# Attention and MLP on one core: a third span's loads into an unused tile, elementwise work moved off GpSimd, a new opening order

## The chip, the core and the metric

The kernel runs on one core of a Trainium2 chip. A core has a matrix engine (TensorE, "PE" in the profile; its weight loads are "PEld"), three engines for elementwise work (VectorE "DVE", ScalarE "ACT", GpSimd "POOL") and SyncE ("SP"), which here only issues DMA transfers. Each engine works through its own queue of instructions in order. The metric is the device time of one execution in microseconds. The median of three runs is 311.8 us (311.51 to 313.07).

## What is computed

Sliding-window attention with a linear bias by distance, then a layer norm and a two-layer MLP with a residual. Batch 8, 8 heads, 576 positions, head size 64, so that a token has 512 features and the MLP 2048 hidden ones.

```
scores = scale * q @ k.T                    # per batch and head, 576 x 576
mask   = (rel >= 0) & (rel < 128)           # rel = query position - key position
attn   = softmax(where(mask, scores - slope[h] * |rel|, -1e9))
x      = heads side by side of (attn @ v)   # 8 x 576 x 512
xn     = (x - mean) / sqrt(var + 1e-6) * g_ln
out    = x + relu(xn @ w_ch1) @ w_ch2
```

## The kernel before, in words

The 4608 tokens are 36 blocks of 128. For a block the kernel turns q and k so that the head size lies on the partitions, makes the scores of the block with itself and with the block before it (line 771), takes the exponential on ScalarE (L819), masks by a product on VectorE (L826) or, for the first five blocks, adds a bias by a matmul beforehand (L787), multiplies with v (L847) and normalizes (L864, L868). The result is layer-normed, turned (L945 on TensorE for the first blocks, DMA transposes later) and enters the MLP as columns of a chunk. Chunks have 3, 3, 2 and then seven times 4 blocks. A chunk's first layer multiplies with w1 (L1244), a relu brings it into `ht` (L1257 on VectorE, L1259 on ScalarE), and the second layer multiplies with w2 (L1278 in the first three chunks). From the fourth chunk on the second layer is made by a seven-product scheme on halves (`seven`: products L1031, sums and differences of h and of the weights L1021 and L991), and in the last two chunks the first layer too (`fours`: products L1160, differences of x L1136, copies of partial results L1171 and L1173, joining additions L1183, a relu in place L1190, a relu from the accumulator L1218). Their sums of weights (L1117) are made late in the run.

`ht` is a ring of two tiles: chunk 0 uses the first, chunk 1 the second, and so on.

**The opening.** q and k of the first six blocks come in three "spans" of two blocks each, as 32-bit values over SyncE's DMA queue (L519): spans 0 and 1 in halves of four heads (256 KB a piece), span 2 as whole pieces (512 KB). They land in `qs` and `ks`, rings of two tiles, so span 2 takes the tiles of span 0 and its load waits until their casts are done. A cast (L666 on ScalarE, L668 on VectorE or GpSimd) makes them 16-bit pairs, TensorE turns them (L686), and VectorE or ScalarE evicts the turned tiles (L695, L697). v (L535) and the weights (L590, L592) come over GpSimd's DMA queue, which casts on the way; each issue is an instruction in GpSimd's own queue, behind its casts. While TensorE has nothing to do in the first 24 us, the program gives it small matmuls on a constant (L1328).

**What sets the order.** The program first lists all work as tasks: the engines that may do a task, a cost for each, dependences, a value `v` that says when it is due. A planner (`Plan.run`) then goes through time, gives every free engine the available task with the lowest value, takes the engine that would end it first where a task may go to several, and emits the instructions in the order found. Tables adjust this by hand: PRI adds to a task's value, HOLD keeps it back until a time, PICK says which engines may take it, QUEUE gives the order of the GpSimd DMA queue and of what is tied to it, and SHARES says how the planner splits the DMA between the two queues. So a change of a table or of one task's engines moves the order on all engines.

The value of a landing tile is a `Ring`: entry k takes tile k modulo the ring's size, its writers wait for the readers of the entry that had the tile before, and an entry can be pinned to a tile of its own:

```
def link(self):
    n = len(self.tiles)
    at = {self.turn(k): k for k in self.first if k not in self.pins}
    for k, tasks in self.first.items():
        if k in self.pins:
            continue
        for t in tasks:
            t.deps += self.readers.get(at.get(self.turn(k) - n), [])
```

Of the kernel before, what the change touches and what calls it, by code (L numbers as in the profile page):

```python
# [10 lines left out]
FP16 = mybir.dt.float16  # L11
FP32 = mybir.dt.float32
AF = mybir.ActivationFunctionType
ALU = mybir.AluOpType
# [41 lines left out]
class Plan:  # L56
# [10 lines left out]
        (True, 512): (0.83, 0.28), (True, 256): (0.75, 0.2), (True, 2048): (0.7, 0.4),  # L67
# [187 lines left out]
def kernel(  # L255
# [86 lines left out]
    mmix = sb("mmix", [P, 4, 2, 2 * P], FP16)  # L342
    mnew = sb("mnew", [P, 4, 2, 2 * P], FP16)
    w1sb = [sb(f"w1sb{m}", [P, NKB, CH], FP16) for m in range(CB)]
    w2sb = [sb(f"w2sb{m}", [P, CB, d_model], FP16) for m in range(CB)]

    single = any(i not in SPANS and i - 1 not in SPANS for i in range(LOAD_CAST))
    q32 = ring("q32", 2, [P, H, D if single else 1], FP32)
    k32 = ring("k32", 2, [P, H, D if single else 1], FP32)
    v32 = ring("v32", min(4, V_CAST), [P, H, D], FP32)  # L350
    qk16 = ring("qk16", 5, [P, 2, d_model], FP16)
    vx = ring("vx", 7 if V_CAST > 4 else 9, [P, H, VD], FP16, FAR)
    qkt = ring("qkt", 6, [P, 2, HP, P], FP16, FAR)
    qs = ring("qs", 2, [P, H, 2 * D], FP32)
    ks = ring("ks", 2, [P, H, 2 * D], FP32)
    qs16 = ring("qs16", 2, [P, H, D, 2], FP16)
    ks16 = ring("ks16", 2, [P, H, D, 2], FP16)
    probs = ring("probs", 3, [P, 4, 2, 2 * P], FP16)
    xb = ring("xb", 4, [P, CB, d_model], FP16)
    xs = ring("xs", 3, [P, d_model], FP16)  # L360
    xt = ring("xt", 3, [P, NKB, CH], FP16)
    ht = ring("ht", 2, [P, NFB, CH], FP16)
    ot = ring("ot", 3, [P, 2, d_model], FP32)
    gcol = sb("gcol", [P, NKB], FP32)
    st = ring("st", 4, [P, nc.vector.BN_STATS_DIM], FP32)
    mv = ring("mv", 4, [P, CB, nc.vector.BN_AGGR_DIM], FP32)
# [148 lines left out]
    def load_span(name, src, r, n, i, v, h0=0, h1=H):  # L515
        (_, _, b, s0), = where(i)

        def emit(e, bank):
            nc.sync.dma_start(  # L519
                out=r[n][:, h0:h1, :],  # L520
                in_=src[b, h0:h1, s0 : s0 + 2 * P, :].rearrange("h (p t) d -> p h (t d)", t=2),
            )
        share = (h1 - h0) / H
        t, d = plan.transfer(f"{name}{i}", "SP", 0.6, 0.05 + 1.7 * share + (0.25 if name in ("qs", "qs0") and i == 0 else 0.0), share, emit, (), v)
        if i < 4:
            d.lat = 1.05 if i else 0.6 if h0 == 0 else 0.9
        r.writes(n, t)
        return d
# [71 lines left out]
    def attention(i):  # L600
# [54 lines left out]
        if i in span_of:  # L655
            n = span_of[i]
            if SPANS[n] == i:
                evs, casts = [[], []], {}
                for (a, x), (landed, h0, h1) in span_load[n].items():
                    r_, w_ = ((qs, qs16), (ks, ks16))[a]  # L660

                    def e_c(e, b, r_=r_, w_=w_, n=n, h0=h0, h1=h1):
                        dst = w_[n][:, h0:h1, :, :].rearrange("p h d t -> p t h d")
                        src = r_[n][:, h0:h1, :].rearrange("p h (t d) -> p t h d", t=2)
                        if e == "ACT":
                            nc.scalar.activation(out=dst, in_=src, func=AF.Copy)  # L666
                        else:
                            (nc.vector if e == "DVE" else nc.gpsimd).tensor_copy(out=dst, in_=src)  # L668
                    f = (h1 - h0) / H
                    cs = add(  # L670
                        f"cT{i}.{a}{x}", pick(f"cs{a}{x}", "POOL", POOL=0.12 + 1.26 * f, ACT=0.22 + 1.18 * f, DVE=0.1 + 0.7 * f),
                        e_c, [landed], av(i, 0.1 * a + 0.2 * x),
                    )
                    r_.reads(n, cs); w_.writes(n, cs)
                    for y in range(2) if f == 1 else (x,):
                        casts[a, y] = cs
# [333 lines left out]
    def seven(c, relu, v0):  # L1010
# [8 lines left out]
        def sums(name, h, out, in0, in1, op, deps, v):  # L1019
            def emit(e, b):  # L1020
                (nc.vector if e == "DVE" else nc.gpsimd).tensor_tensor(out=out, in0=in0, in1=in1, op=op)  # L1021
            return add(f"{name}{c}.{h}", pick1(name, 2 * c + h, "DVE", DVE=0.69, POOL=1.45), emit, deps, v)
# [83 lines left out]
    def first_sums():  # L1106
# [3 lines left out]
        for m in range(2):  # L1110
# [4 lines left out]
            for n, (dst, x, y, op) in enumerate(((s1, a21, a22, ALU.add), (s2, s1, a11, ALU.subtract), (a21, a11, a21, ALU.subtract), (s4, a12, s2, ALU.subtract))):  # L1115
                def emit(e, b, dst=dst, x=x, y=y, op=op):
                    (nc.vector if e == "DVE" else nc.gpsimd).tensor_tensor(out=dst, in0=x, in1=y, op=op)  # L1117
                need = prev[-1:] + scaled[m :: 2] + free
                if n == 2:
                    need = need + plain_all[m + 2]  # L1120
                prev.append(add(f"sumW{m}.{n}", pick1("sumW", 2 * n + m, "POOL DVE", DVE=0.75, POOL=1.45), emit, need, FIRST[BOTH] / CB * SPAN - BEFORE - 12.0 + n))
# [247 lines left out]
```

## Time and profile before

| what | before |
|---|---|
| median of three runs | 311.8 us (311.51 to 313.07) |
| the profiled execution's own time | 312.74 us |
| its span, first to last instruction | 311.0 us |
| mean granted TensorE clock | 0.992 |
| first w1 matmul (L1244) starts | 26.65 us |
| busy in 235 to 291 us: PE, DVE, ACT, POOL | 53.40, 44.15, 22.62, 20.62 of 56 us |
| relus in place (L1190): GpSimd, VectorE | 10 of 1562 ns, 14 of 342 ns |
| differences of x (L1136): GpSimd, VectorE | 6 of 1272 and 1378 ns, 2 of 400 ns |
| loads of q and k spans, 256 KB, issue to landing | 4.9 and 4.6 us |
| load of the third span's k, 512 KB | 10.4 us |

The page cuts the span into 40 slices of 7.8 us and gives for each engine the busy share in tenths (9 is 90% or more); PEclk is the clock that TensorE was granted, in tenths of full speed. A row of a timeline has the start, the duration, the engine, the line, the operation, its output and input, how many instructions are merged, and in brackets how long the engine had stood before it and what ended that. A row of the chain has the start, the time spent and what was waited for or done. A row of waits has who waited for whom, the time in all, the number of waits and the longest. In the table of stretches each engine's busy time is followed by its count of instructions; the last three columns are the granted clock, the DMA share and GB/s.

### The profile page before, as it was taken

The page shows a single profiled execution, that of the slowest core. Times are in us where ns is not written, and L with a number is a line of the kernel's source. Part 1 is how long each engine was busy: PE and PEld are TensorE (multiplying, and loading weights), DVE is VectorE, ACT ScalarE, POOL GpSimd, SP SyncE. Part 2 cuts the span into 40 slices and gives each one's busy share as a digit, 9 for nine tenths or more (in the row PEclk, how much of TensorE's full clock was granted, in tenths as well). Part 3 has the DMA queues.
Part 4 walks back from the last instruction along what each step waited for, and adds up shares of the span by engine and source line. Part 5 has one row for each costly group of instructions (what it writes and reads, how often), then busy time and mean ns, then how long its engine had stood idle before and what let it go on. Part 6 is the DMA issues. An engine that isn't in the chain of part 4 may idle for free.

```text
span 311.0 us, 7474 instructions
## 1 busy us (share of the span) xinstructions
PE 299.4 (96%) x2985; PEld 220.5 (71%) x2985; DVE 246.2 (79%) x588; ACT 165.3 (53%) x276; POOL 124.6 (40%) x149
## 2 busy tenths in 40 slices
PE   8797999999999999999999999999999999989995
PEld 7574655765685558856876578667876689988884
DVE  3395669998898469965995999999999598966963
ACT  2573933885692783586266875586527532343100
POOL 2919467678541764354256152000302451323100
PEclk9997999999999999999999999999999999999999
DMA  7999999999999999999999999911040100300043
GB/s 200 239 209 207 195 163 105 197 131 174 164 186 146 211 128 118 142 185 179 152 129 169 204 168 149 227 34 36 3 157 14 35 2 0 115 23 2 15 156 102
DMA packets 156485, 40.21 MB, mean 129 GB/s; under 512 B 142625, under 2 KB 151841, under 8 KB 156450
## 3 DMA queue, kind: packets, MB, share of 16 engines
q0 software_dynamic: 101680, 16.65, 83.5%
q1 hardware_dynamic: 54768, 23.08, 39.0%
q8 instruction: 23, 0.38, 0.5%
q14 instruction: 12, 0.10, 0.1%
q10 hardware_dynamic: 2, 0.00, 0.0%
HBM read 36.70 MB, written 9.44 MB: 148 GB/s over the span
## 4 chain that ended last, share of the span: by engine, by line
PE 89%; DMA 5%; DVE 2%; POOL 1%; ACT 1%; SPq 1%; issue 1%; POOLq 0%; DVEq 0%; ACTq 0%
PE fb L1244 32%; PE fb L1031 27%; PE fb L1278 9%; PE sc L1160 7%; PE sc L771 6%; PE fb L847 5%; DMA ks<-in_k_dram 3%; DMA qs<-in_q_dram 2%; DVE ht L1183 2%; PE fb L734 1%; PE fb L686 1%; ACT probs L1173 1%; POOL ks L668 1%; SPq L519 0%; PE fb L465 0%
## 5 line engine op out<-in xcount | busy, mean ns | idle before, releaser
L1244 PE MATMUL fb<-xt,w1sb 128*128 128x512 f16 (+2 forms) x512 | 107.5, 357 | 0.0
L819 ACT ACTIVATE probs<-sc 128x1024 f16<-128x1024 f32 (+1 forms) x72 | 67.6, 974 | 33.3 <-PE sc L771 33.1
L1259 ACT ACTIVATE ht<-fb 128x512 f16<-128x512 f32 (+2 forms) x112 | 61.1, 552 | 39.9 <-PE fb L1244 35.1
L1244 PEld LDWEIGHTS <-w1sb 128*128 128x128 f16 x512 | 55.2, 115 | 33.7 <-issue 1.5
L1031 PEld LDWEIGHTS <-ht 128*128 128x128 f16 x560 | 53.3, 98 | 7.4
L535 POOL DMA_DIRECT2D vx<-in_v_dram x36 | 30.6, 853 | 50.4 <-PE fb L847 41.7
L1031 PE MATMUL fb<-w2sb,ht 128*128 128x256 f16 x336 | 42.5, 273 | 0.0
L1190 POOL TENSOR_SCALAR ht<-ht 128x512 f16<-128x512 f16 x10 | 15.6, 1562 | 49.3 <-DVE ht L1183 31.8
L535 POOL DMA_DIRECT2D qk<-in_k_dram x34 | 29.3, 867 | 13.2 <-DMA qkt<-qk 8.1
L535 POOL DMA_DIRECT2D qk<-in_q_dram x34 | 28.7, 848 | 11.6 <-DMA qkt<-qk 6.1
L826 DVE TENSOR_TENSOR probs<-probs,mreg 128x1024 f16<-128x1024 f16 (+1 forms) x46 | 30.8, 674 | 2.8 <-ACT mreg L497 2.7
L1278 PE MATMUL fb<-w2sb,ht 128*128 128x512 f16 x128 | 30.9, 379 | 0.0
L847 PEld LDWEIGHTS <-probs 128*128 128x128 f16 x544 | 24.7, 97 | 8.3
L868 DVE SCALAR_TENSOR_TENSOR xb<-fb,rec 128x256 f16<-128x256 f32 x72 | 29.3, 415 | 0.9
L1031 PE MATMUL fb<-ks,ht 128*128 128x256 f16 x224 | 27.8, 273 | 0.0
L847 PE MATMUL fb<-vx,probs 128*128 128x65 f16 x496 | 27.4, 193 | 0.0
L887 DVE BATCH_NORM_STATS2 st<-xb 128x6 f32<-128x512 f16 x36 | 24.7, 686 | 0.2
L864 DVE RECIPROCAL rec<-fb 128x4 f32<-128x4 f32 x72 | 12.2, 173 | 15.1 <-PE fb L847 14.4
L1183 DVE TENSOR_TENSOR ht<-sc,probs 128x512 f16<-128x512 f32 x24 | 16.3, 688 | 8.9 <-PE sc L1160 5.4
L1173 ACT ACTIVATE probs<-sc 128x512 f32<-128x512 f32 x23 | 13.3, 596 | 17.9 <-PE sc L1160 13.9
L1042 DVE TENSOR_TENSOR ot<-fb,xb 128x512 f32<-128x512 f32 (+1 forms) x31 | 19.5, 634 | 3.2 <-PE fb L1031 2.9
L771 PEld LDWEIGHTS <-qkt 64*128 64x128 f16 x496 | 14.8, 94 | 7.7 <-issue 5.6
(117 smaller groups left out, 407.9 us busy)
## 6 DMA issues: line engine op xcount, KB each, us to landing
out_dram<-ot SPq DMA_DIRECT2D x32, 256.0 KB, 3.5
vx<-in_v_dram POOLq DMA_DIRECT2D x28, 128.0 KB, 6.8
qk<-in_q_dram POOLq DMA_DIRECT2D x26, 128.0 KB, 6.9
qk<-in_k_dram POOLq DMA_DIRECT2D x26, 128.0 KB, 7.7
w1sb<-in_moe_w_ch_dram POOLq DMA_DIRECT2D x4, 512.0 KB, 9.7
w2sb<-in_moe_w_ch_dram POOLq DMA_DIRECT2D x4, 512.0 KB, 10.2
qs<-in_q_dram SPq DMA_DIRECT2D x4, 256.0 KB, 4.9
ks<-in_k_dram SPq DMA_DIRECT2D x4, 256.0 KB, 4.6
```

The costliest lines, as they stand in the source:

```text
L535: nc.gpsimd.dma_start(out=dst(p0, n), in_=src[b, :, s0 : s0 + n, :].rearrange("h p d -> p h d"))
L771: nc.tensor.matmul(scs[half][:, g, c0 : c0 + P], kt[rows, 1, hp, :], qkt[i][rows, 0, hp, :], start=not bias, stop=True, skip_group_check=True,
L819: nc.scalar.activation(out=o, in_=n_, func=AF.Exp, scale=inv_sqrt_d)
L826: en.tensor_tensor(out=pv, in0=pv, in1=mask[:, 2 * half : 2 * half + 2, :, lo:], op=ALU.mult)
L847: nc.tensor.matmul(pp[:, hh * (D + 1) : hh * (D + 1) + D + 1], probs[i][:, bank, slot, side * P : side * P + P], vx[i if side else before] ...
L868: nc.vector.scalar_tensor_tensor(out=xb[c][:, j, 256 * half : 256 * half + 256].rearrange("p (h d) -> p h d", d=D), in0=pp[:, :, 0:D], sca ...
L887: nc.vector.bn_stats(out=st[i][:, :], in_=xb[c][:, j, :])
L1031: nc.tensor.matmul(o, lhs(f, p), rhs(f), start=first and f == 0 and (p == 0 or key[0] != key[1]), stop=f == F2 - 1, skip_group_check=True)
L1183: nc.vector.tensor_tensor(out=o, in0=bank.rearrange("p (f c) -> p f c", f=2), in1=other.rearrange("p (f c) -> p f c", f=2), op=ALU.add)
L1244: nc.tensor.matmul(fb[b][:, 0:n_], w1f[f // CB][:, kb, f % CB, :], xt[c][:, kb, 0:n_], start=(kb == 0), stop=(kb == NKB - 1),)
L1259: nc.scalar.activation(out=ht[c][:, f, 0:n_], in_=src, func=AF.Relu)
L1278: nc.tensor.matmul(pm[:, 0 : c1 - c0], ht[c][:, f, j * P : j * P + P], w2sb[f // CB][:, f % CB, c0:c1], start=(f == 0), stop=(f == NFB - 1),)
```

## The change

Three edits in the code, and new tables.

1. `ht` is made before `qs` and `ks`, and these two rings get a pin: their entry 2, the third span, lies in the second tile of `ht` (as 32-bit values, q in its first quarter and k in its second). The third span's loads count as writers and its casts as readers of an entry -1 of `ht`, so that the first writers of that tile (chunk 1's relus) wait for them.
2. The sums and differences (`sums` in `seven`, `first_sums`, the differences of x in `fours`) can only go to VectorE, and the relu in place goes to ScalarE or VectorE, where it went to GpSimd or VectorE. `sums` in `seven` and `first_sums` had run on VectorE already.
3. SHARES for small packets beside weight pieces goes from (0.83, 0.28) to (0.84, 0.16), and PRI, HOLD, PICK and QUEUE are new throughout.

```
@@ SHARES
-        (True, 512): (0.83, 0.28), (True, 256): (0.75, 0.2), (True, 2048): (0.7, 0.4),
+        (True, 512): (0.84, 0.16), (True, 256): (0.75, 0.2), (True, 2048): (0.7, 0.4),
@@ QUEUE
-QUEUE = ['cT0.00', 'v2', 'v1', 'w0', 'v3', 'cT2.01', 'w4', 'v4', 'w1', 'w2', 'cT4.10', 'dist2', 'w3', 'w5', 'w6', 'dist1b', 'v5', 'q6', 'k6', 'w7']
+QUEUE = ['cT0.00', 'dist00', 'v2', 'iden2', 'v1', 'w3', 'cT2.10', 'v3', 'w0', 'v5', 'w1', 'v4', 'w2', 'w4', 'cT4.10', 'dist2', 'w5', 'dist1b', 'q6', 'k6', 'w6', 'w7']
@@ rings
-    qs = ring("qs", 2, [P, H, 2 * D], FP32)
-    ks = ring("ks", 2, [P, H, 2 * D], FP32)
+    ht = ring("ht", 2, [P, NFB, CH], FP16)
+
+    def early(n):
+        return ht.tiles[1][:, 4 * n : 4 * n + 4, :].rearrange("p f c -> p (f c)").bitcast(FP32).rearrange("p (h d) -> p h d", h=H)
+
+    qs = plan.ring([sb(f"qs{n}", [P, H, 2 * D], FP32) for n in range(2)], {2: early(0)})
+    ks = plan.ring([sb(f"ks{n}", [P, H, 2 * D], FP32) for n in range(2)], {2: early(1)})
...
-    ht = ring("ht", 2, [P, NFB, CH], FP16)
@@ load_span
         r.writes(n, t)
+        if n == 2:
+            ht.writes(-1, t)
@@ the span's casts
                     r_.reads(n, cs); w_.writes(n, cs)
+                    if n == 2:
+                        ht.reads(-1, cs)
@@ sums in seven
-                (nc.vector if e == "DVE" else nc.gpsimd).tensor_tensor(out=out, in0=in0, in1=in1, op=op)
-            return add(f"{name}{c}.{h}", pick1(name, 2 * c + h, "DVE", DVE=0.69, POOL=1.45), emit, deps, v)
+                nc.vector.tensor_tensor(out=out, in0=in0, in1=in1, op=op)
+            return add(f"{name}{c}.{h}", ("DVE", 0.69), emit, deps, v)
@@ differences of x in fours
-                (nc.vector if e == "DVE" else nc.gpsimd).tensor_tensor(out=dst, in0=x, in1=y, op=ALU.subtract)
-            t = add(f"tx{c}.{n}", pick1("tx", 4 * c + n, "DVE POOL", DVE=0.42, POOL=0.8), emit, done + prev[1:2] + prev[0:1] + x_use[c % 2] + masked, v0 - 6.0 + n)
+                nc.vector.tensor_tensor(out=dst, in0=x, in1=y, op=ALU.subtract)
+            t = add(f"tx{c}.{n}", ("DVE", 0.42), emit, done + prev[1:2] + prev[0:1] + x_use[c % 2] + masked, v0 - 6.0 + n)
@@ relu in place
-                        (nc.vector if e == "DVE" else nc.gpsimd).tensor_scalar(out=o, in0=o, scalar1=0.0, scalar2=None, op0=ALU.max)
-                r_ = add(f"r{name}{c}.{u}", pick1("r" + name, 4 * c + u, "POOL DVE", POOL=0.75, DVE=0.25, ACT=0.6), emit_r, [t], vu + n * step - 4.0)
+                        nc.vector.tensor_scalar(out=o, in0=o, scalar1=0.0, scalar2=None, op0=ALU.max)
+                r_ = add(f"r{name}{c}.{u}", pick1("r" + name, 4 * c + u, "ACT DVE", ACT=0.6, DVE=0.32), emit_r, [t], vu + n * step - 4.0)
```

`first_sums` is edited like `sums` (its cost becomes 0.72 on VectorE). The numbers in `add` are the planner's costs, by which it orders the work; they are no measurements.

By the compiled order of instructions, the GpSimd queue of the opening reads after the change: a cast of span 0's k, v of block 2, the identity, v of block 1, w1's fourth quarter, v of block 3, w1's first, v of block 5, w1's second, v of block 4, w1's third, w2's first, the cast of the third span's k, w2's second, and on. SyncE's queue reads: q and k of span 0 (k in two pieces), v of block 0, q of span 0, q of span 1, k of span 2, k and q and k of span 1, q of span 2. TensorE's stream has 76 of the small constant matmuls ahead of the first turn and 34 more in the opening.

## Prediction

> **What bounds the kernel now.** I read the page first, then the chain of waits in order of time, then TensorE's timeline where that chain leaves TensorE, and last the waits of the final stage.
>
> Page: busy shares, TensorE's row of slices, and the granted clock.
>
> ```profile
> PE 299.4 (96%) x2985; PEld 220.5 (71%) x2985; DVE 246.2 (79%) x588; ACT 165.3 (53%) x276; POOL 124.6 (40%) x149
> ...
> PE   8797999999999999999999999999999999989995
> ...
> PEclk9997999999999999999999999999999999999999
> ```
>
> TensorE is full from slice 5 (31 us) almost to the end. An edit can win only in the first four slices, where the clock also dips, or in the final stage (235 to 291 us). The other engines are hidden between. The chain names what held the opening:
>
> ```profile
> 12.53 0.78 POOL ks L668
> 13.32 10.40 DMA ks<-in_k_dram
> 23.87 1.33 POOL ks L668
> ...
> 26.86 4.04 PE fb L1244 x16
> ...
> 33.99 3.90 PE fb L1244 x24
> ```
>
> The third span's k is issued only at 13.32, when a GpSimd cast has freed its buffer; beside the weight loads it takes 10.40 us, and a GpSimd cast of 1.33 follows. TensorE's timeline at that place:
>
> ```profile
> 22.70 0.39 PE L686 MATMUL fb<-iden,qs 128*128 128x128 f32 x2
> 25.25 0.44 PE L686 MATMUL fb<-iden,ks 128*128 128x128 f32 x2 [2.16 <-POOL ks L668]
> 25.52 0.39 PE L945 MATMUL fb<-iden,xs 128*128 128x128 f16 x4
> ```
>
> TensorE stands 2.16 us at the third span's turn (L686). Behind it in the queue is the turn of block 2's x (L945), the last thing that the first MLP chunk needs. The first w1 matmul starts at 26.65. Then the clock, in the table of stretches:
>
> ```profile
> 26.25:29.66 3.41, 3.41 (x14) 1.84 (x13) 3.33 (x11) 1.58 (x4) 3.41 (x6) 0.50 1.24 205
> ```
>
> 0.50 is the granted clock: half speed for 3.41 us, right after the hole. By the chain's rows 16 matmuls took 4.04; at the pace of the later 24 (3.90) they take 16 x 0.1625 = 2.60. Price of the half clock: **1.44 us**.
>
> **The change, part by part.**
>
> *Third span into the second h tile.* In the new instruction order no load of SP waits for a cast any more: k of the third span is SP's seventh load, then the rest of span two, then q. The only new wait is the first relu into that h tile, which now waits for the two casts. By its place in ScalarE's order that relu comes after 55 us, the casts end near 20: nothing, and without that cover it would cost what the casts are late.
>
> When do they land? The rows of the first casts show one 256 KB share after the other: 6.04 (third), 7.19 (fourth), 8.13 (fifth), 8.99 (sixth), 0.92 apart. Seven shares follow: alone, the last lands at 8.99 + 7 x 0.92 = 15.4. They aren't alone. GpSimd's first cast now takes the third share (6.04) instead of the fifth (8.13), so its v and weight loads begin 2 us sooner (issue 7.1 for 8.79); their first packets came at 12.0, so now about 10.3. By then SP has moved some (10.3 - 2) x 278 GB/s = 2.3 of 3.4 MB. 1.1 MB is left, beside the software queue. The DMA view of before gives packets and megabytes by queue (q1 is SP's, q0 GpSimd's), first for 5 to 11 us, then for 17 to 19, then for 17 to 23:
>
> ```profile
> q1 hardware_dynamic: 3808, 1.67, 119.1%
> ```
>
> ```profile
> q0 software_dynamic: 633, 0.19, 87.4%
> q1 hardware_dynamic: 518, 0.27, 58.7%
> ```
>
> ```profile
> q0 software_dynamic: 1599, 0.76, 94.5%
> q1 hardware_dynamic: 1022, 0.52, 40.5%
> ```
>
> Alone SP's queue moves 278 GB/s, beside v and a little weight 0.27 MB in 2 us (133), beside all 0.52 in 6 (87). So q lands between 15.4 (no sharing) and 10.3 + 1.1/0.087 = 23; with 133, since two v loads stand at the front of GpSimd's queue, 18.6. I take **18.8**, with a little for the last lane.
>
> *Opening laid anew.* GpSimd does 2 of the spans' casts instead of 4, VectorE 6 instead of 4 (0.45 each), ScalarE 5 turn evictions instead of 2 (0.60 each), and the identity on GpSimd now stands behind its first cast and the first v load. I followed the new order with durations from the rows. VectorE's identity copy (0.42) sits behind the cast of the sixth share (8.99 + 0.46), so the first turn starts at 9.9 (8.94 before). ScalarE then runs: span two's q cast when that share lands (12.6 to 13.6), block 0's two exponentials (to 14.7), an eviction (15.3), block 1's two (1.02 each, after their scores at about 15.9) to 18.0, then the third span's q cast (1.35). So that cast starts at max(18.0, landing), and **behind it in ScalarE's queue stand block 2's exponentials**. From the cast's start to the first w1 matmul: cast 1.35, exp 2 x 0.55, scores of block 3 behind them on TensorE 1.3, exp 1.02, eviction 0.5, exp 1.02, two evictions 1.1, semaphores 0.2: 7.6 us. Checked against before: cast at 15.36, block 2's x ready at 23.25, and turn and eviction would allow 24.4 without the hole; that is 9.0, in which one exponential (1.02) now stands ahead of the cast: 8.0. The first w1 matmul starts at 18.8 + 7.6 = **26.4, against 26.65: -0.25**. The hole is gone, but the attention chain in front is later by nearly as much. What is late next is ScalarE.
>
> The weights come in another order: v, v, w1's last quarter, v, its first, v, its second, v, its third. Up to the second of these quarters that is 1.45 MB (0.13 a v, 0.52 a quarter): at 95 GB/s beside SP's queue (0.19 MB in 2 us) until 18.8, then at some 208 alone (25 to 31 us), it is in at 21.9, the next quarter at 25.1, the last at 28.2. In TensorE's order they are needed at 26.4, some 4 us later, and some 8 us later: nothing, with over 4 us of cover.
>
> *The clock.* Between 22.84 and 26.25 TensorE was busy 1.25 us; now some 3 us of small work lies there, since the turns no longer stand. I take the half clock away: **-1.44**. Against it, TensorE's warm-up matmuls (76 before the first turn) end near 7.6 and the first turn is at 9.9: a hole of 2.3 us, of the size that brought half clock. Small matmuls of about 2.4 us would double there, and 18.0 - 18.8 hides some: 0 to +1.6, which I reckon in the chances alone, but for the rounding below.
>
> [...]
>
> *Elementwise work on h off GpSimd.* Final stage, waits list, TensorE's own:
>
> ```profile
> PE sc L1160 <- DVE ht L1183: 1.1, 3, 0.5
> ...
> PE sc L1160 <- ACT probs L1173: 1.0, 3, 0.4
> ...
> PE sc L1160 <- ACT ht L1218: 0.5, 1, 0.5
> ```
>
> 2.6 us is all there is. GpSimd's ten relus (1562 ns each) and six subtractions go: by the new order 15 of 24 relus are ScalarE's, 9 VectorE's (14 before), all 8 subtractions VectorE's (2 before), as are 3 copies instead of 1. VectorE: 6 x 0.40 + 2 x 0.69 - 5 x 0.34 = +2.1; ScalarE +15 x 0.60 (no row of a relu in place; the nearest is L1218, 597 ns) - 2 x 0.60 = +7.8, in a stage where it is busy 22.6 of 56. And VectorE is slowed beside GpSimd:
>
> ```profile
> 253.77 1.60 POOL L1136 TENSOR_TENSOR qkt<-xt,qkt 128x512 f16<-128x512 f16 x1
> ...
> 254.28 1.64 DVE L1021 TENSOR_TENSOR ht<-ht 128x1024 f16<-128x1024 f16 x1
> ```
>
> Alone this form takes 0.68. L1021's four groups (means 750, 746, 725, 690, x14) lose 2.7 us to that over the run. VectorE nets -0.6: nothing to either side by itself. The waits can go (-2.6) or double (+2.6), as the order of short steps falls; I take **-0.4**, near nothing, since the rows nearly cancel.
>
> **Sum.** -0.25 - 1.44 - 0.4 = -2.1 against the profiled execution's own time of 312.74 (span 311.0, 1.74 around it): 310.6. It stands 0.94 over the median of the runs, so 311.8 - 2.1 = 309.7; I round to **309.9** for the uncosted hole.
>
> **Rivals.** 0.5% of 311.8, 1.56 us, is about what a measurement of this kernel can tell from no change.
>
> 1. *Forecast*: 309.9, own range 308.7 to 311.1. Chance 0.42. About 0.27 of it is faster by over 0.5%, 0.15 within.
> 2. *More is won*: q lands by 18.0 (first w1 matmul at 25.6, -1.05), half clock gone, half to all of the final waits too (-1.3 to -2.6): 311.8 - 3.8 to 5.1 = 306.7 to 308. For it: alone the loads would be in by 15.4. Against: the 10.40 of the same load beside weights. 0.20.
> 3. *Slower, q too late*: at 87 GB/s it lands at 23, and ScalarE stands with block 2's exponentials behind it. First w1 matmul at 23 + 7.6 = 30.6, +4.0, and TensorE has its hole again, so the half clock stays: +4.0 - 0.4, 315.4. It turns slower by 0.5% from a landing at 21.0 (28.6: +1.95, less 0.4). For it: 133 to 87 GB/s is a small step. 0.20, 313.4 to 315.4.
> 4. *Nothing is won*: the new hole of 2.3 us at 7.6, or a wait for q at 20, calls half clock, and -1.44 falls away: 311.2, 310.2 to 313. 0.18: 0.12 within, 0.06 slower.
>
> Faster: 0.27 + 0.20 = 0.47. Same: 0.15 + 0.12 = 0.27. Slower: 0.20 + 0.06 = 0.26. The range leaves out about a tenth at each end: 306.7 to 314.3.
>
> **What the changed profile would show.** Right: no wait of TensorE for the third span's cast, ScalarE's 1024-wide cast starting near 19, the first w1 matmul at 25.5 to 27, PEclk 0.9 or more in slice 4. ScalarE idle for the DMA of q beyond 20 speaks for rival 3; half clock anywhere before 30 us for rival 4. In the final stage: TensorE's three waits at about 2 us in all and VectorE's 128x1024 additions all near 0.68. Wrong would make me above all the share that SP's queue gets beside GpSimd's, and any wait of TensorE for a weight piece after 27 us.

## The result, and the profile after

The changed kernel is **slower**: 315.65 us (median of four runs, 314.98 to 315.97) against 311.65 (311.29 to 313.07) of the kernel before in the same session, ratio 1.012 with a 95% interval from 1.008 to 1.015. Its profiled execution took 315.51 us, 313.5 of it span.

Page of the kernel after: busy shares and granted clock.

```profile
PE 301.0 (96%) x2992; PEld 221.2 (71%) x2992; DVE 246.6 (79%) x595; ACT 169.8 (54%) x287; POOL 100.4 (32%) x131
...
PEclk9789999999999999999999999999999999999999
```

The engines do what the change says: GpSimd falls from 124.6 to 100.4 us, VectorE stays. The dip of the clock has not gone: it stands in the second slice now. TensorE's timeline there, then ScalarE's:

```profile
9.56 0.44 PE L694 MATMUL fb<-iden,qs 128*128 128x128 f32 x2 [2.60 <-DVE iden L448]
...
11.46 2.07 PE L469 MATMUL fb<-ot 1*128 1x512 f32 x2
...
28.23 2.11 PE L1252 MATMUL fb<-xt,w1sb 128*128 128x384 f16 x12 [0.26 <-ACT xt L963]
```

```profile
13.56 0.60 ACT L476 ACTIVATE g_t<-fb 128x512 f32<-128x512 f32 x1 [2.71 <-PE fb L469]
...
19.24 1.94 ACT L827 ACTIVATE probs<-sc 128x1024 f16<-128x1024 f32 x2 [1.84 <-PE sc L779]
...
21.06 1.35 ACT L672 ACTIVATE qs<-ht 128x1024 f16<-128x1024 f32 x1
```

Lines of the new kernel lie 4 or 8 further down (L469 is the old L465, L694 the old L686, L1252 the old L1244). Three things are to be seen. TensorE stands 2.60 us ahead of the first turn, for the identity's copy on VectorE. The two matmuls of g (L469) take 2.07 us instead of 1.12. And ScalarE reaches its cast of the third span's q only at 21.06, straight from block 1's exponentials, without a wait for the load; the first w1 matmul follows at 28.23 instead of 26.65. The table of stretches has the clock:

```profile
11.02:17.85 6.83, 6.83 (x39) 3.94 (x37) 3.06 (x6) 2.94 (x5) 6.48 (x9) 0.50 1.51 218
```

Half speed for 6.83 us right after the new hole, full speed from 17.85 on, so that the w1 matmuls run at their pace from the first on (12 in 2.11 us). In the final stage the waits list has, for TensorE:

```profile
PE sc L1168 <- DVE ht L1191: 2.7, 5, 0.9
PE sc L1168 <- ACT probs L1181: 1.1, 4, 0.3
```

That is 3.8 us in nine waits, where before had 2.6 in seven.

**Where the time is lost.** I take the starts of all matmuls in both traces, and for each moment of the kernel before the work of TensorE that is still to come (each matmul at the usual distance of its form). The changed kernel reaches the same remaining work later by 0.2 us at 31 us, by 0.4 at 236, and by 2.1 from 290 on. From the start of the last matmul to the end of the span it takes 4.1 us instead of 3.8, and 2.05 lie outside the span instead of 1.70. So 315.51 - 312.74 = 2.8 is: opening 0.2, middle 0.2, **final stage 1.7**, end 0.7. The opening loses so little because the first w1 matmul is 1.6 late, but the 1.44 of the old half clock is regained. Of the final stage's 1.7 the waits list shows 1.2; the rest lies in matmuls that start later beside these waits. The other 1.1 us of the medians' difference is the base: the profiled execution of before (312.74) lies that much over the median of 311.65.

### The profile page after: what moved, and what is told of

It is laid out like the page before. It is cut to its first block, busy times and chain, and to the rows that moved or that the text cites. A ratio compares the mean times of both kernels' runs of the same rounds, so it can differ in the third digit from the quotient of the medians.

```text
span 313.5 us, 7484 instructions
## 1 busy us (share of the span) xinstructions
PE 301.0 (96%) x2992; PEld 221.2 (71%) x2992; DVE 246.6 (79%) x595; ACT 169.8 (54%) x287; POOL 100.4 (32%) x131
## 4 chain that ended last, share of the span: by engine, by line
PE 88%; DVE 6%; ACT 2%; DMA 2%; issue 1%; SPq 1%; DVEq 0%; ACTq 0%
PE fb L1252 31%; PE fb L1039 27%; PE fb L1286 9%; PE sc L1168 7%; PE sc L779 6%; PE fb L855 5%; DMA qs<-in_q_dram 2%; DVE ht L1191 1%; DVE xb L876 1%; SPq L523 1%; ACT probs L1181 1%; PE fb L742 1%; PE fb L694 1%; PE fb L469 1%; DVE ot L1050 0%
## 5 line engine op out<-in xcount | busy, mean ns | idle before, releaser
L1252 PE MATMUL fb<-xt,w1sb 128*128 128x512 f16 (+2 forms) x512 | 107.0, 353 | 0.3 <-ACT xt L963 0.3
L1252 PEld LDWEIGHTS <-w1sb 128*128 128x128 f16 x512 | 54.8, 114 | 32.9 <-issue 0.3
L1039 PEld LDWEIGHTS <-ht 128*128 128x128 f16 x560 | 52.8, 98 | 7.7
L541 POOL DMA_DIRECT2D vx<-in_v_dram x36 | 30.6, 850 | 56.6 <-PE fb L855 51.6
L855 PEld LDWEIGHTS <-probs 128*128 128x128 f16 x544 | 25.1, 98 | 8.5 <-ACT probs L827 0.4
L1286 PE MATMUL fb<-w2sb,ht 128*128 128x512 f16 x128 | 30.9, 379 | 0.1
L1039 PE MATMUL fb<-ks,ht 128*128 128x256 f16 x224 | 28.5, 273 | 0.0
L1286 PEld LDWEIGHTS <-ht 128*128 128x128 f16 x128 | 11.6, 97 | 11.0 <-issue 0.2
L1181 ACT ACTIVATE probs<-sc 128x512 f32<-128x512 f32 x21 | 12.1, 596 | 12.6 <-PE sc L1168 11.3
```

What stands on the lines that cost most here:

```text
L541: nc.gpsimd.dma_start(out=dst(p0, n), in_=src[b, :, s0 : s0 + n, :].rearrange("h p d -> p h d"))
L855: nc.tensor.matmul(pp[:, hh * (D + 1) : hh * (D + 1) + D + 1], probs[i][:, bank, slot, side * P : side * P + P], vx[i if side else before] ...
L1039: nc.tensor.matmul(o, lhs(f, p), rhs(f), start=first and f == 0 and (p == 0 or key[0] != key[1]), stop=f == F2 - 1, skip_group_check=True)
L1252: nc.tensor.matmul(fb[b][:, 0:n_], w1f[f // CB][:, kb, f % CB, :], xt[c][:, kb, 0:n_], start=(kb == 0), stop=(kb == NKB - 1),)
L1286: nc.tensor.matmul(pm[:, 0 : c1 - c0], ht[c][:, f, j * P : j * P + P], w2sb[f // CB][:, f % CB, c0:c1], start=(f == 0), stop=(f == NFB - 1),)
```

## The experiments

Eighteen kernels. In all of them, the two bases included, the 54 transposing DMAs (none before 59 us) are plain DMA copies of the same tiles, so x, q and k of the later blocks are not transposed; every engine's other instructions and their order stay. In the snippets `e` is the engine and `t` the task at the place where the program emits the planned order; to change `e` there moves one instruction to another engine without moving anything else.

**Two bases.** Before and after, each with

```
-                    nc.sync.dma_start_transpose(out=xt[c][:, :, y * P : y * P + P], in_=xs[x][:, :])
+                    nc.sync.dma_start(out=xt[c][:, :, y * P : y * P + P], in_=xs[x][:, :].rearrange("p (kb c) -> p kb c", kb=NKB))
```

and the same for `qkt`.

> The base of the runs that follow: the kernel before, whose 54 transposing DMAs of x, q and k (from 62 us on) are plain DMA copies of the same tiles, so that x, q and k of the later blocks are not transposed; every other instruction and every engine's order is as before. All of them are hidden beside TensorE's work by the trace, so the time should stay: 311.3 to 312.1 us. Rival (a transposing DMA sets the time somewhere in the middle): 310 us or less.

Measured: 311.57 us (310.67 to 313.34), 0.998 of before (0.995 to 1.001). As expected.

> The changed kernel with the same plain copies in place of its transposing DMAs. Expected as c_before: 315.0 to 316.1 us. Rival: the changed kernel's loss hangs on those transfers, 313 us or less.

Measured: 315.62 us (314.79 to 316.13), 1.0105 (1.007 to 1.014). As expected. So both may stand for the kernels.

**The pinned tile alone.**

```
-                out=r[n][:, h0:h1, :],
+                out=(early(0 if name[0] == "q" else 1) if n == 2 else r[n])[:, h0:h1, :],
```

> c_before with one thing of the change alone: the third span's q and k land in the second h tile, every engine's order as before. The pinned tile by itself is a gain (theory): k of the third span is no longer issued at 13.32 but right behind SP's other loads, lands 2 to 4 us before 23.7, TensorE's stand of 2.16 us shrinks to under 0.5, the first w1 matmul comes at 24.5 to 25.5 instead of 26.65 and the half clock after 26 us goes: 309 to 310.5 us, against 311.7. Rival (the attention chain in front of block 2's x holds the first w1 matmul all the same): it stays at 26.3 to 26.7, only the half clock may go, 310.5 to 311.7 us. Second rival (third span beside the other loads takes their share): the second span's pieces land later, the first w1 matmul is at 27 or later, over 311.7 us.

Measured: **310.16 us** (309.77 to 310.54), 0.992 (0.990 to 0.995). Here lines lie 4 further than in before.

```profile
17.14 1.40 POOL L672 CAST ks<-ht 128x1024 f16<-128x1024 f32 x1
...
25.31 2.76 PE L1248 MATMUL fb<-xt,w1sb 128*128 128x384 f16 x16
```

The cast of the third span's k starts at 17.14, with no wait for the load, instead of 23.87. The stand of 2.16 us is gone, the first w1 matmul starts at 25.31, and the 16 matmuls that took 4.04 take 2.76. Eight of nine executions were granted 0.998 or more. The first reason of the prediction was right, and the edit is a gain by itself; the loss is in the rest of the change. Its own base is c_before, though, whose profiled execution (310.67) stood only 1.41 us at this turn, had no half clock behind it, and had its first w1 matmul at 26.15. The two profiled executions are 0.8 apart (310.67 and 309.84), which is the earlier start; the rest of the 1.4 in the medians is clock: of c_before's twelve executions only four were granted 0.998 or more (310.73 to 311.57).

**The final stage alone.** The change's code for `first_sums`, the differences of x and the relu in place, with its PICK, PRI and HOLD for that stage, in the kernel before; from 215 us on, every engine's order is that of the change.

```
-            t = add(f"tx{c}.{n}", pick1("tx", 4 * c + n, "DVE POOL", DVE=0.42, POOL=0.8), emit, ...
+            t = add(f"tx{c}.{n}", ("DVE", 0.42), emit, ...
...
-                r_ = add(f"r{name}{c}.{u}", pick1("r" + name, 4 * c + u, "POOL DVE", POOL=0.75, DVE=0.25, ACT=0.6), emit_r, ...
+                r_ = add(f"r{name}{c}.{u}", pick1("r" + name, 4 * c + u, "ACT DVE", ACT=0.6, DVE=0.32), emit_r, ...
```

> c_before with the change's final stage alone (relus and differences of x off GpSimd, the change's tables for this stage). Theory that the final stage costs what the trace shows there: 1.5 to 1.9 us more than before, 313.2 to 313.6 us, with TensorE's waits on sc near 3.8 us instead of 2.6. Rival (the stage's loss in the changed kernel only follows from its late opening): 311.5 to 312 us, waits as before.

Measured: 315.07 us (312.34 to 317.77), 1.007 (1.003 to 1.010): the stage costs in the kernel before too, by the median more than expected. Of this kernel's executions the three with a granted 0.998 or more took 312.34 to 313.48, against 310.73 to 311.57 of c_before's four: about 2.2. At equal remaining work its trace falls back by 2.06 us between 236 and 290 us. The clock of the opening varies in this kernel and the median mixes both; behind the opening of c_before_pin, with the same edit, it is quiet:

> c_before_pin (310.16 us) with the whole of the change's final stage, its order and its engines. From c_before and c_before_tail, whose final stages differ by 2.06 us in their traces: 312.0 to 312.6 us.

Measured: 312.33 us (312.20 to 314.10), 2.2 over c_before_pin. As expected.

**Engines or order?** First the engines alone, in the old order.

```
+            if e == "POOL" and t.name[:2] == "rj":
+                e = "ACT"
```

> c_before_pin (310.16 us) with GpSimd's ten relus of the final stage on ScalarE, each at its old place in the order of the program; the differences of x stay on GpSimd. Queue theory (a relu that waits for VectorE's addition stands ahead of the copies out of PSUM on ScalarE, and these free sc): TensorE's waits on sc grow from 2.6 to 4 us or more, 311.5 to 313 us. Rival (it is the change's own order of the stage, not the engine): 309.9 to 310.5 us.

Measured: 309.95 us (309.81 to 310.25). My theory of ScalarE's queue fell: the waits are those of c_before_pin to the digit.

```profile
PE sc L1164 <- DVE ht L1187: 1.1, 3, 0.5
PE sc L1164 <- ACT probs L1177: 1.0, 3, 0.4
PE sc L1164 <- ACT ht L1222: 0.5, 1, 0.5
```

```
+            if e == "POOL" and t.name[:2] in ("rj", "tx"):
+                e = "DVE"
```

> c_before_pin (310.16 us) with GpSimd's ten relus and six differences of the final stage on VectorE, each at its old place in the order of the program. VectorE gets 10 x 0.29 + 6 x 0.42 = 5.4 us more, loses the slow additions beside GpSimd (about 2 us), and no relu waits there for another engine. Queue theory: about the same, 309.5 to 311 us. Rival (VectorE's additions, which free sc, come late behind the added work): 311.5 to 313 us.

Measured: 311.16 us (310.86 to 311.69), 1.0 over c_before_pin. The profiled executions are 1.4 apart: 0.2 in the opening, 0.5 in the stage, 0.3 from the last matmul to the end, 0.35 outside the span. Then the order alone, with the engines put back:

```
+            if e == "ACT" and t.name[:3] in ("rja", "rjb", "rjc") or t.name in ("tx8.0", "tx8.2", "tx9.0", "tx9.1", "tx9.2", "tx9.3"):
+                e = "POOL"
```

> pin_tail with the change's order of the final stage kept, but ScalarE's relus and six of the eight differences of x on GpSimd, each at its place in that order. Order theory (the stage's new order costs by itself, since the relus on ScalarE cost nothing in the old order and all ten relus and six differences on VectorE cost 0.5 us there): 311.8 to 313 us. Rival (the engines cost, in this order): back to 310 to 310.8 us.

Measured: 312.40 us (312.11 to 313.06). **The order costs the whole of it**, whoever does the relus. (GpSimd does 15 relus here, ten in the kernel before; the change's copies and its nine relus on VectorE stay. TensorE's order is that of pin_tail, instruction by instruction.) The timeline of pin_tail shows the longest of the waits:

```profile
247.22 0.60 PE L1164 MATMUL sc<-xt,mnew 128*128 128x256 f16 x4
...
247.68 0.60 PE L1164 MATMUL sc<-xt,w1sb 128*128 128x256 f16 x4
...
248.12 0.60 PE L1164 MATMUL sc<-qkt,w1sb 128*128 128x256 f16 x4
...
248.75 1.29 DVE L1187 TENSOR_TENSOR ht<-sc,probs 128x512 f16<-128x512 f32 x2 [0.35 <-PE sc L1164]
...
250.09 0.60 PE L1164 MATMUL sc<-qkt,mmix 128*128 128x256 f16 x4 [0.94 <-DVE ht L1187]
```

Three products into sc follow each other; two of VectorE's additions come after the third; the next product needs the sc tile that they free (there are two). Only four matmuls of the other kind (L1035, at 248.55) stand before it. In c_before_pin eight of them follow the second product:

```profile
247.04 0.60 PE L1164 MATMUL sc<-xt,w1sb 128*128 128x256 f16 x4 [0.25 <-ACT probs L1177]
...
247.43 1.28 DVE L1187 TENSOR_TENSOR ht<-sc,probs 128x512 f16<-128x512 f32 x2
247.47 1.04 PE L1035 MATMUL fb<-w2sb,ht 128*128 128x256 f16 x8
```

Is it the tables' doing? The kernel before has twelve entries for this stage, which the change drops. Put back into pin_tail:

```
+PRI:  'Ub8.2': -2.4, 'rjb8.2': 2.0, 'jc8.2': -3.7, 'Pg8.00': -5.4, 'Ua9.0': 7.1, 'jc9.0': 2.1, 'Pa9.10': -1.7, 'Pd9.11': 13.0, 'Pf9.10': -1.5, 'rg9.1': -4.0
+HOLD: 'rc7.0': 255.17, 'Ua9.3': 274.86
```

> pin_tail (312.33 us: the change's final stage behind the pinned opening) with before's twelve table entries for the final stage put back; relus and differences stay on ScalarE and VectorE. Tables theory (the order is worse because its tuned entries are gone): 310 to 311 us. Rival (the planner's order follows from the engines and their costs, the entries do little): 312 to 312.6 us.

Measured: 313.76 us (313.19 to 314.31): neither of the two, it makes things worse. Taken out of c_before_pin (the same lines with a minus):

> c_before_pin (310.16 us) with those twelve entries taken out, relus and differences on GpSimd as before. Tables theory: 311.3 to 312.5 us. Rival: 310 to 310.6 us.

Measured: 310.07 us (309.91 to 310.74): nothing. So the order comes out of the planner as soon as the relus and differences carry other engines and costs, and these twelve entries don't repair it; other entries weren't tried.

**The opening.** First each suspected wait by itself, on c_after. The hole:

```
-        for _ in range(int((b - a + more - 0.06) / (0.11 if a < 4.5 else 0.06))):
+        for _ in range(int((b - a + more - 0.06) / (0.11 if a < 4.5 else 0.06)) + (40 if a < 2.0 else 0)):
```

> c_after (the changed kernel with plain copies for its transposing DMAs) with 40 more warm-up matmuls ahead of the first turn, which fill the hole of 2.6 us at 7 us. Clock theory (this hole calls the half clock of 11 to 18 us, and that delays the opening): no half clock before 20 us, the 1x512 matmuls of g back at 1.1 us, first w1 matmul at 26.5 to 27.2 instead of 28.2, 313.9 to 314.6 us against 315.6 of c_after. Rival (q of the third span lands at 20.9 and holds ScalarE's cast with block 2's exponentials behind it): clock full, but the first w1 matmul at 27.9 to 28.2, 315.2 to 315.7 us.

Measured: 315.60 us (314.28 to 317.34); no gain in the median, and a wider spread. The median is the rival's, but not for its reason, which was a w1 matmul that stays where it was. In its profiled execution (317.34, the latest of the six) the early half clock is gone and the matmuls of g take 1.12, but the first w1 matmul comes at 29.95:

```profile
18.30 0.45 DVE L674 CAST ks<-ks 128x512 f16<-128x512 f32 x1 [3.95 <-DMA ks<-in_k_dram]
```

```profile
19.11 0.38 PE L855 MATMUL fb<-vx,probs 128*128 128x65 f16 x4 [2.99 <-DVE qktp L703]
...
29.95 2.11 PE L1252 MATMUL fb<-xt,w1sb 128*128 128x384 f16 x12 [0.26 <-ACT xt L963]
```

VectorE waits 3.95 us for the second span's last piece, which lands near 18; the eviction behind that cast (L703, at 18.64) frees a tile in PSUM (where all matmuls of these kernels write), and TensorE stands 2.99 us for it. Half clock follows this stand, from 19.13 on. Next, q's landing:

```
-QUEUE = ['cT0.00', 'dist00', 'v2', 'iden2', 'v1', 'w3', 'cT2.10', 'v3', 'w0', 'v5', ...
+QUEUE = ['cT0.00', 'dist00', 'v2', 'iden2', 'v1', 'cT2.10', 'v3', 'w3', 'w0', 'v5', ...
```

> c_after with one move in GpSimd's queue: the first weight load (w1's last quarter) is issued behind the identity copy's successors and the v load that followed it, two places later, so that q of the third span shares less. Landing theory: q lands at 18 to 19.5 instead of 20.9, and since ScalarE is free for its cast only then, the first w1 matmul comes at 26.5 to 27.5 instead of 28.2: 314 to 315 us. Rival (ScalarE itself is busy until 21 with block 1's exponentials, which the half clock has made late): q lands earlier, its cast still starts at 21, first w1 matmul at 28.0 to 28.3, 315.4 to 315.8 us.

Measured: 315.76 us (315.56 to 316.85). The last packets of q land at 18.84 instead of 20.04 in c_after, and ScalarE's cast still starts at 21.36 (21.29 in c_after). The rival was right. Then, on c_after_warm, the third span's k behind the second span's last piece:

```
+    one = order.pop(at.index("ks4.i"))
+    at = [t.name for t, e, b in order]
+    order.insert(at.index("ks1.2.i") + 1, one)
```

> c_after_warm (changed kernel, hole at 7 us filled) with one move in SP's queue: the third span's k is issued behind the second span's last piece instead of ahead of its last three. Queue theory (with k ahead of them, the second span's last piece lands at 14.4 to 18.2 us; VectorE's cast waits for it, the turn eviction behind that cast keeps a PSUM bank, and TensorE stands up to 3 us behind that bank): the piece lands at 13 to 14.5, TensorE's wait of 2.99 at 19 us is gone, first w1 matmul at 26.3 to 27.5 instead of 29.95, 313.2 to 314.3 us, runs within 1.5 us of each other instead of 3. Rival (the order of ScalarE's work, block 1's exponentials and the third span's cast behind block 0's, holds the opening by itself): first w1 matmul at 27.5 to 28.5, 314.5 to 315.3 us.

Measured: 316.88 us (314.33 to 319.32), neither of the two. The piece lands at 11.8, its cast runs at 14.00 without a wait for it, and the wait of 2.99 us is gone. ScalarE has ended block 1's exponentials at 17.8, and now stands itself:

```profile
21.24 1.34 ACT L672 ACTIVATE qs<-ht 128x1024 f16<-128x1024 f32 x1 [3.41 <-DMA ht<-in_q_dram]
```

This is the wait that the prediction's rival 3 named. All three at once, on c_after_warm_k (w1's pieces w3 and w0 both go behind the next two v loads, further back than in c_after_land):

```
-QUEUE = ['cT0.00', 'dist00', 'v2', 'iden2', 'v1', 'w3', 'cT2.10', 'v3', 'w0', 'v5', 'w1', ...
+QUEUE = ['cT0.00', 'dist00', 'v2', 'iden2', 'v1', 'cT2.10', 'v3', 'v5', 'w3', 'w0', 'w1', ...
```

> c_after with all three at once: hole at 7 us filled, third span's k behind the second span's last piece in SP's queue, and GpSimd's first two weight loads behind its next two v loads. Theory of stacked waits (half clock, the second span's last piece, q's landing at 21 each hold the same chain, and hide each other): q lands by 18.8, ScalarE's cast of it starts at 18 to 19 instead of 21.2, first w1 matmul at 25.8 to 27, 313 to 313.8 us (the final stage's 2 us stay). Rival (the order of TensorE's and ScalarE's work in the new opening holds it even then): first w1 matmul over 27.5, 314.5 us or more.

Measured: **313.19 us** (312.58 to 314.83), 2.4 less than c_after, with a granted clock of 0.997 or more in all twelve executions.

```profile
18.53 1.35 ACT L672 ACTIVATE qs<-ht 128x1024 f16<-128x1024 f32 x1
...
25.69 2.11 PE L1252 MATMUL fb<-xt,w1sb 128*128 128x384 f16 x12 [0.26 <-ACT xt L963]
```

q lands at 18.4, its cast starts at 18.53, the first w1 matmul at 25.69. Block 1's scores are made from 16.27 here, from 18.80 in the kernel after. Three waits were stacked on one chain, and the removals that were tried short of all three (the hole, q's landing, the hole with the piece) showed nothing or a loss. That all three are needed is not shown: the piece alone, and the other two pairs, were not run. With before's final stage as well (the diff of c_before_tail turned round, `sums` too), the account closes:

> c_after_all3 (313.19 us) with before's final stage as well (relus and differences on GpSimd, before's tables there). If the parts add up: 313.19 - 2.1 for TensorE's waits on sc - 0.6 (the end behind the last addition and the time outside the span, both longer in kernels whose GpSimd is idle in the final stage) = 310.3 to 311.3 us, below before. Rival (the final stage's loss depends on how the opening runs): 312 us or more.

Measured: 310.20 us (309.88 to 311.71), 0.994 (0.992 to 0.997), just under what was expected, although 0.3 of the 0.6 expected at the end was gone already: c_after_all3 has only 1.7 us outside its span. Between the two profiled executions (312.61 and 310.05) the stage makes 2.5 and the end 0.3. It is also the time of the tile alone (310.16): even with its waits gone, the rest of the new opening wins nothing over the old one.

**What is good in the new opening.** The opposite direction, on c_before_pin:

```
+    one = order.pop(at.index("ks4.i"))
+    at = [t.name for t, e, b in order]
+    order.insert(at.index("ks0.2.i"), one)
```

> c_before_pin (310.16 us) with the same move the other way: the third span's k is issued ahead of the second span's last three pieces, as the change has it. Queue theory: the second span's last piece lands 1 to 3 us later than 13.24, its casts and turns and block 2's scores with it, first w1 matmul at 26 to 27.5 instead of 25.31, 310.9 to 312.3 us. Rival (these casts have room, the order of the other engines is what costs): first w1 matmul at 25.2 to 25.7, 309.9 to 310.5 us.

Measured: 310.42 us (309.98 to 311.23), first w1 matmul at 25.95. The time is the rival's, the first w1 matmul lies between the two: the third span's k ahead of the second span's pieces costs at most 0.3 us where the rest has room, and the ranges (309.77 to 310.54 there) overlap. Then GpSimd's loads sooner:

```
+            e = {"cT0.00": "DVE", "cT0.10": "POOL"}.get(t.name, e)
```

> c_before_pin (310.16 us) with two of the first casts swapped between GpSimd and VectorE (GpSimd casts the third share, VectorE the fifth), so that GpSimd's v and weight loads are issued at 6.9 instead of 8.8 us, as the change has it. Landing theory: SP's last loads share from 9 on, q of the third span lands at 18 to 20.5 instead of 16.0, ScalarE's cast waits for it, first w1 matmul at 26.5 to 28.5 instead of 25.31, 311.3 to 313.5 us. Rival: q lands at 16 to 17, 310 to 310.6 us.

Measured: **308.62 us** (308.34 to 309.12), 0.989 (0.987 to 0.991): the fastest median of all kernels here.

```profile
8.74 0.44 PE L690 MATMUL fb<-iden,qs 128*128 128x128 f32 x2 [0.70 <-DVE qs L672]
...
14.74 1.35 ACT L670 ACTIVATE qs<-ht 128x1024 f16<-128x1024 f32 x1 [0.43 <-DMA ht<-in_q_dram]
...
23.87 2.76 PE L1248 MATMUL fb<-xt,w1sb 128*128 128x384 f16 x16
```

The first w1 matmul starts 1.44 us sooner, which neither of the two expected. My theory of the sharing holds for k, not for q. GpSimd's loads are issued at 6.91; in this kernel SP's last load is the third span's k, and it lands at 20.74 instead of 16.04 in c_before_pin. GpSimd waits for it, its cast runs from 20.90 to 22.24, and k's turn on TensorE starts at 22.30, so it comes just in time. q stands one place ahead of k and is in 0.43 us after ScalarE is free. What is won: VectorE's cast of the fifth share takes 0.45 instead of GpSimd's 0.75, the first turn comes 0.6 us sooner, and the chain with it. And a wait of c_before_pin for GpSimd's casts, which come sooner too, is gone:

```profile
13.73 0.44 PE L690 MATMUL fb<-iden,ks 128*128 128x128 f32 x2 [0.78 <-POOL ks L672]
```

The same line on c_before:

> c_before (311.57 us) with the two first casts swapped between GpSimd and VectorE, without the pinned tile. Theory that the swap wins by itself (first turn 0.6 us sooner, GpSimd's later casts 1 us sooner, the ks buffer free sooner, k issued near 12 instead of 13.32): first w1 matmul at 25 to 25.8, 310 to 311 us. Rival (it needs the pinned tile; without it k lands at 23 or later beside weights that come sooner, TensorE stands at the third span's turn again): 311.3 to 313 us.

Measured: 308.88 us (308.08 to 313.44), 0.988 (0.984 to 0.991). The swap wins without the tile too, but not every time: five of eight executions took 308.1 to 309.1, three 312.3 to 313.4. In the profiled one (313.44) the third span's q is issued at 8.81, behind a cast, and ScalarE stands for it with exponentials behind:

```profile
18.61 1.33 ACT L666 ACTIVATE qs<-qs 128x1024 f16<-128x1024 f32 x1 [4.25 <-DMA qs<-in_q_dram]
```

TensorE stands 4.08 us for these exponentials and gets half clock from 19.19. This is rival 3's wait again, in the kernel without the tile. In pin_gps_early, with the tile, q is issued at 7.11 and cast at 14.74, and all executions are quick; that the tile is what keeps the wait away in each of them is not shown. The five quick executions here (median 308.4) are as fast as pin_gps_early.

## Why the prediction was wrong, point by point

- **Third span into the h tile: right.** No load of SP waits any more, the old hole and the half clock behind it are gone, and alone the edit brings 1.4 us in the medians (311.57 to 310.16).
- **The whole.** The sum gave 310.6 for the profiled execution, and it took 315.51, 4.9 more: 1.8 in the opening (first w1 matmul at 28.23 for 26.4), 0.2 in the middle, 2.1 in the final stage (+1.7 for -0.4), 0.7 at the end, a term that the sum doesn't have. Two steps failed, ScalarE's cast in the opening and the final stage.
- **"I take the half clock away: -1.44": half right.** It did leave the w1 matmuls. The new hole ("0 to +1.6, which I reckon in the chances alone") came as rival 4 has it, at 2.60 us, and called 6.83 us of half clock where I had priced one stretch of small matmuls. What I missed is not the doubled small matmuls but who waits for them: ScalarE stands 2.71 us for g's two matmuls, and all of its chain moves. Its price is small, as far as one execution tells: the only one of c_after at a granted 1.0 took 314.79, the other five 315.43 to 316.13, about 0.9 us.
- **"So that cast starts at max(18.0, landing)": the failing step of the opening.** Both terms were too low: ScalarE was there at 21.06 instead of 18.0, q landed at 20.89 instead of 18.8. In this execution ScalarE came last, by 0.2, but q alone would have cost nearly as much. SP's queue had moved 2.36 MB by 10.6 us, as summed; the other 1.05 MB took until 20.89, 102 GB/s where the sum took 133. From the cast to the first w1 matmul it took 7.17 us, near the 7.6 of the sum. Where the two terms were brought back (c_after_all3: 18.53), the first w1 matmul came at 25.69, against a forecast of 26.4. ScalarE's 18.0 was summed from the durations of its own queue, with block 1's scores ready at about 15.9. But they were made only from 18.80, since TensorE in its own order had g and the second span's turn ahead of them, at half clock; and in c_after_warm TensorE in turn waited for a PSUM tile behind a cast that waited for a DMA. (A small slip in the lower bound: the rows 6.04 to 8.99 are 0.98 apart, not 0.92, which makes 15.9 of 15.4.)
- **Weights: right in the outcome.** The second, third and fourth of w1's quarters to come landed at 24.1, 27.5 and 30.9 instead of 21.9, 25.1 and 28.2; the cover of 4 us held, and TensorE waited for none.
- **"Final stage, -0.4 (near nothing, since the rows nearly cancel)": the failing step of the final stage, and the largest term: +1.7**, and 0.7 at the end, which the prediction put at nothing. I had weighed the engines' loads. These cost 0 to 0.5 us in the old order. The new order costs 2.1 by itself, and I had it in the compiled order without following it: which product into sc comes directly behind which.
- **The base.** Of the 101 executions of before in these sessions two took about 316. Of the other 99, the 26 with a granted clock of 0.998 or more have a median of 311.33 us, the 73 others one of 312.94. The profiled execution (312.74 at 0.992) is like those 73: the half clock behind the hole, whose 1.44 the sum takes off, was read from it. Taken off the median of the three runs (311.8), only 0.5 over the quicker kind, most of it was not there to be won.

Rival 3 (slower, q too late) named 313.4 to 315.4, and 315.65 was measured, but that is luck. Its sum has the first w1 matmul at 30.6 and half clock there; they were 28.23 and none, and 2.4 us of the loss (stage and end) lie where it has -0.4. ScalarE did not stand for q in the kernel after, which was rival 3's sign; it did in c_after_warm_k. The sign that the changed profile does show is rival 4's, half clock before 30 us from the new hole. I had given the two chances as if only one could hold, and the final stage, where most was lost, was in neither.

## What to carry to other kernels

When a chain has several waits, take them all away at once before you call any of them harmless: here the two single removals and the one pair that were tried gained nothing, and the three together 2.4 us. Where a planner makes the order, an edit of costs or engines must be judged by the order that comes out, instruction by instruction at the narrowest buffer (here the two sc tiles in PSUM), and not by the engines' loads; to keep the order and move only the engine tells the two apart in one run. Split a bundle into its parts: the tile (-1.4 us), and one swapped pair of casts (-1.5 more on top of it), were gains that two other parts of the same change had eaten. Such gains don't add up: the swap without the tile brings 2.7 in the median, both together 2.95.

## What the runs showed of the hardware

- **Half clock followed the stretches of 3.41 us in which TensorE was least busy, not the longest stands.** Every stretch of half clock in the openings lasts 3.41 or 6.83 us. They start at 10.92 (c_before), 11.02 (after), 11.36 (c_after_land), 11.63 (c_after), 12.22 (pin_k_ahead), 19.13 (c_after_warm), 19.19 (before_swap), 23.02 (c_after_warm_k), 26.25 (before) or 26.42 us (c_before_tail), and full speed first starts anywhere from 4.1 to 7.3 us after the span's start (5.77 in before, 4.20 in after, 4.80 in c_after, whose opening is the same). In before full speed then lasts 20.48 us (5.77 to 26.25), in after 6.83 (4.20 to 11.02): six and two times 3.413. The length of a stand doesn't tell whether half clock follows: stands of 2.57 to 2.96 us in c_after and c_after_land were followed by half clock, and so were one of 1.71 in pin_k_ahead (10 of 12 executions at 0.994) and one of 1.44 in c_before, while one of 1.53 in c_before_pin was not (8 of 9 at 0.998 or more). What separates them is how much of such a stretch TensorE was busy. In before it was 1.25 of 3.41 us, a share of 0.37, in the one ahead of the half clock:

```profile
22.84:26.25 3.41, 1.25 (x20) 1.00 (x19) 1.28 (x5) 0.32 (x2) 2.38 (x4) 1.00 1.38 203
```

  If all twenty traces are cut into stretches of 3413 ns, counted from the first change of the clock to some 8 us before the end, and g's two matmuls of one row are not counted as busy, the 14 stretches with a share up to 0.51 are each followed by half clock, and the 1719 others, from 0.535 on, all by full speed. (In before 0.37 is followed by half clock, and the lowest share followed by full speed is 0.66; in after these are 0.30 and 0.44, and 0.71.) That matmuls of one row don't count is fitted to this (with them five of the 14 have shares of 0.75 to 1.0); no run isolates it.
- **Two casts at once.** VectorE's cast of 128x512 took 1.90 us at 16.32 in the kernel after, beside GpSimd's cast of 16.57 to 17.92, and 1.72 in c_after_land, where they also meet (16.81 and 16.86). It took 0.45 in c_after_warm, where they don't, and 0.44 in c_after, where it ends before GpSimd's begins (17.05). But casts of this size also took 0.64 to 0.80 in c_after_all3 with no GpSimd cast beside them, so the cause is not isolated.
- **The end is longer where GpSimd is silent.** From the start of the last matmul to the end of the span it is 4.06 to 4.14 us in the ten kernels whose GpSimd has nothing to do in the final stage, and 3.79 to 3.81 in the ten others, before among them, where it keeps at least the differences. Outside the span it is 2.0 to 2.2 in the changed kernel, c_after, its first three variants and pin_all_dve, and 1.7 in all others. That it goes with GpSimd's work and not with the order is seen in pin_tail (4.06) and pin_tail_pool (3.79), whose TensorE has the same order. The cause of neither is settled.
